# Relative-bias attention and a snake MLP on one core: first loads in another order, and each engine's order of work from a table

## The chip, the core and the metric

The kernel runs on one core of a Trainium2 chip. The core has a matrix engine (TensorE, PE in the profile, with its weight loads on a row of their own, PEld), a vector engine (VectorE, DVE), an engine for activation functions (ScalarE, ACT), a general one (GpSimd, POOL) and one that issues transfers (SyncE, SP). Each engine takes its instructions in the order in which the program holds them, and they meet through semaphores. The metric is device time in microseconds (us), lower is better.

## What is computed

Attention over 8 batches, 8 heads, 576 positions and 64 dimensions, with a bias that depends on the distance of two positions through a table of 32 buckets; its output, seen as 4608 tokens of 512 features, goes through two matrix products with a snake function between them.

```python
scores = scale * np.matmul(q, k.transpose(0, 1, 3, 2))
bucket = np.where(is_small, n, large)          # of n = |i - j|
scores = scores + bias_table[bucket].transpose(2, 0, 1)[None]
attn = np.exp(scores - np.max(scores, axis=-1, keepdims=True))
attn = attn / (np.sum(attn, axis=-1, keepdims=True) + 1e-09)
x = np.matmul(attn, v)                         # heads side by side: 4608 x 512
h = x @ w_in                                   # 512 -> 2048
g = h + np.sin(alpha * h) ** 2 / (alpha + 1e-09)
out = g @ w_out                                # 2048 -> 512
```

## The kernel before

**Attention.** For a batch t the heads are taken in four pairs p. Scores of a pair are matmuls with 64 rows of contraction, the two heads in the two halves of the array (L1069 the main ones, L1059, L1035 and L1030 for the last 64 positions). ACT makes the exponential of 128x1024 scores at a time (`exp_u`, L1076), DVE multiplies in the bias near the diagonal as a factor (`band_t`, L1097; `band_x`, L1081 and L1084), PE multiplies with v over the whole array (`av`, L1111 and L1120), DVE divides by the sum of the exponentials (`norm`, L1130 and L1131). The result is turned into `xT`, in batch 0 by PE (`turn_x_pe`), later by a transposing transfer on SP's queue (`turn_x`, L1137).

**The two products.** The 4608 tokens are cut into nine blocks of 480 to 576, without regard to the batches, so a block needs the finished `xT` of one or two batches. For each block and each of 16 slices of the 2048 features: `moe_in` (four matmuls over the whole array, L1163), the sine on ACT (L1170), square and `g` on DVE (L1174, L1188). Then `moe_out` for each 128 tokens: 16 matmuls (L1197), cut into eight pieces of two, `evict` on DVE (L1203), `store` on SP (L1206). Scores and exponentials of later batches are laid between the pieces of `moe_out`.

**The start.** The first pair of batch 0 comes in halves of its positions: `first_load` (L844) brings two halves of k on SP's queue and two of q on ACT's queue in 32 bit, `first_cast` makes 16 bit of them, `turn_half` turns each on PE with the identity matrix (L990), `half_copy` copies the turned half out of PSUM (L1002, `kT` and `qT`). All other pairs of batches 0 and 1 come on POOL's queue already cast (`load_nat`, L884) and are turned by `turn` (L1010) and copied by `turn_copy` (L1020 on DVE, L1018 on ACT). The bias needs the table (`load_tab`, L863) and constants (`load_consts`, L860); `bias_sub` on PE (L930), `bias_exp` on ACT (L934), `bias_sel` on DVE (L937), four small matmuls (L943), `bias_copy` on ACT (L948), and then eight transfers that spread it out (L958, four on SP's queue, four on POOL's). From batch 2 on, k is written to HBM in 16 bit (L911) and read back transposed (`turn_staged`, L917); of q the same from batch 3.

**What sets the order.** All work is a list of some 1,700 tasks with dependencies, an engine, a duration, and a priority. `_Plan.run` plays it through: whenever an engine is free, it takes from that engine's ready tasks the one of the lowest priority number. The order in which the tasks start in this play is the order in which they are emitted, and so each engine's fixed order of instructions; PSUM banks are given out on the way. Tasks of a named sequence (`seq`) keep the order in which they were added.

The lines on which the start depends, in `_graph`:

```python
first[kind][half] = add("ACT" if kind else "SP", 0.45, E("first_load", kind, half),
                        lat=3.4 if half else 2.95, prio=-9 + 0.3 * half)
t_id = add("SP", 0.45, E("load_ident"), lat=2.7, prio=-8.9)
t_cst = add("ACT", 0.45, E("load_consts"), lat=4.4, prio=-8)
t_tab = add("SP", 0.45, E("load_tab"), lat=4.0, prio=-8)
```

Of the kernel before, what the change touches and what calls it, by code (L numbers as in the profile page):

```python
# [117 lines left out]
class _Plan:  # L118
# [8 lines left out]
    def __init__(self):  # L127
        self.tasks = []
        self.nseq = {}
        self.banks = _Banks()  # L130
        self.fill = None
        self.FILL = 0.0

    def add(self, *a, **kw):
        t = _Task(*a, **kw)
        t.idx = len(self.tasks)
        if not t.lat and not t.pipe:
            t.lat = self.LAT.get(t.eng, 0.0)
        if t.seq is not None:
            t.sn = self.nseq.get(t.seq, 0)  # L140
            self.nseq[t.seq] = t.sn + 1
        self.tasks.append(t)
        return t
# [33 lines left out]
    def run(self):  # L177
# [4 lines left out]
        nxt_seq = {}  # L182
# [11 lines left out]
        n = len(self.tasks)  # L194
        order = []
        while n:
            moved = False
            nxt = None
            for e, cand in pool.items():
# [4 lines left out]
                for t in cand:  # L204
                    if t.seq is not None and nxt_seq.get(t.seq, 0) != t.sn:
                        continue
# [48 lines left out]
                t = best  # L255
# [23 lines left out]
                cand.remove(t)  # L279
                for a in after.get(t.idx, ()):  # L280
                    left[a.idx] -= 1
                    if not left[a.idx]:
                        pool[a.eng].append(a)
# [48 lines left out]

def _graph(K, opt):
    plan = _Plan()
    plan.FILL = opt["fill"]
    plan.fill = lambda m, i: K.fill(m, i)
# [18 lines left out]
    for half in range(2):  # L355
        for kind in range(2):
            first[kind][half] = add("ACT" if kind else "SP", 0.45, E("first_load", kind, half),
                                    lat=3.4 if half else 2.95, prio=-9 + 0.3 * half)
    t_id = add("SP", 0.45, E("load_ident"), lat=2.7, prio=-8.9)
# [148 lines left out]
    def turn_first():  # L508

        done = [[None, None], [None, None]]  # L510
        for half in range(2):
            for kind in range(2):
# [3 lines left out]
                a.emit = lambda a=a, cell=cell, kind=kind, half=half: K.turn_half(cell, tag(a), kind, half)  # L516
                act = (kind, half) in opt["h_act"]
# [10 lines left out]
    def turn(t, p):  # L528
        cell = {}
        for kind in range(2):  # L530
# [5 lines left out]
            a.emit = lambda a=a, kind=kind: K.turn(cell, tag(a), t, p, kind)  # L536
            act = kind and t == 0 and p in opt["turn_act"] or t and (p, kind) in opt["act1"]
# [216 lines left out]
    c_act=((1, 1),), h_act=(), p_bias=-0.5, nu=12, ng=3, first=(1, 1, 1), bs=2, win=7, hold={3:  # L754
# [9 lines left out]
class _Ops:  # L764
# [91 lines left out]
    def load_ident(self):  # L856
        self.nc.sync.dma_start(out=self.ident, in_=self.ident_h.ap())
# [401 lines left out]
```

## Time and profile before

| what | value |
|---|---|
| time, three runs | 393.79, 396.3 and 396.61 us, median 396.3 |
| span of the profiled execution, first to last instruction | 391.7 us |
| TensorE clock granted over the span | 0.994 of full speed |
| busy in the span: PE, DVE, ACT, POOL | 374.0, 301.1, 279.8, 86.4 us |
| matmuls of `moe_in` and `moe_out` | 640 and 576 |
| exponentials of 128x1024 | 160, 154.4 us on ACT |

The profile doesn't say which of the three times belongs to the profiled execution. Its span lies 2.1 us under the lowest and 4.6 us under the median; what lies around the span is between these.

How to read it: busy time of PE is modelled for the ends of matmuls, which overlap, so a stretch that shows 100% may still have small gaps. In the chain of waits a piece runs from the start of its instructions to the start of the next piece, so a gap shows there as a longer piece.

### The profile page before, as it was taken

The page shows a single profiled execution, that of the slowest core. Times are in us where ns is not written, and L with a number is a line of the kernel's source. Part 1 is how long each engine was busy: PE and PEld are TensorE (multiplying, and loading weights), DVE is VectorE, ACT ScalarE, POOL GpSimd, SP SyncE. Part 2 cuts the span into 40 slices and gives each one's busy share as a digit, 9 for nine tenths or more (in the row PEclk, how much of TensorE's full clock was granted, in tenths as well). Part 3 has the DMA queues.
Part 4 walks back from the last instruction along what each step waited for, and adds up shares of the span by engine and source line. Part 5 has one row for each costly group of instructions (what it writes and reads, how often), then busy time and mean ns, then how long its engine had stood idle before and what let it go on. Part 6 is the DMA issues. An engine that isn't in the chain of part 4 may idle for free.

```text
span 391.7 us, 9363 instructions
## 1 busy us (share of the span) xinstructions
PE 374.0 (95%) x3811; PEld 201.1 (51%) x3811; DVE 301.1 (77%) x738; ACT 279.8 (71%) x339; POOL 86.4 (22%) x101
## 2 busy tenths in 40 slices
PE   3979979999999999999999999999999999999996
PEld 2557435565446545564466445644664454444442
DVE  6498797777987798769976997798669889778221
ACT  2888876989689978887789769987897964333000
POOL 8695744080008000900080004000000000000000
PEclk9999998999999999999999999999999999999999
DMA  9999999999549924997499329600211001101122
GB/s 165 197 170 183 195 184 149 145 170 165 82 97 168 176 14 91 165 167 57 89 179 153 34 66 204 74 19 28 64 44 42 30 19 46 36 27 56 54 82 80
DMA packets 148171, 40.80 MB, mean 104 GB/s; under 512 B 134416, under 2 KB 143456, under 8 KB 148128
## 3 DMA queue, kind: packets, MB, share of 16 engines
q0 software_dynamic: 96656, 18.45, 57.7%
q1 hardware_dynamic: 50912, 21.25, 27.9%
q8 instruction: 30, 0.49, 0.5%
q10 hardware_dynamic: 560, 0.50, 0.4%
q14 instruction: 13, 0.11, 0.1%
HBM read 36.94 MB, written 15.93 MB: 135 GB/s over the span
## 4 chain that ended last, share of the span: by engine, by line
PE 88%; DVE 8%; DMA 2%; ACT 1%; issue 1%; SPq 0%
PE acc L1197 33%; PE acc L1163 29%; PE acc L1120 9%; PE acc L1069 9%; DVE g L1188 3%; PE acc L1111 2%; PE acc L1030 2%; PE acc L1059 2%; DMA toep<-in_k_dram 2%; DVE u L1097 1%; DVE s L1174 1%; PE acc L1010 1%; PE acc L1035 1%; DVE xp L1131 1%; DVE qT L1020 1%
## 5 line engine op out<-in xcount | busy, mean ns | idle before, releaser
L1076 ACT ACTIVATE u<-acc 128x1024 f16<-128x1024 f32 x160 | 154.4, 1024 | 21.2 <-PE acc L1069 9.7
L1197 PE MATMUL acc<-w_out,g 128*128 128x512 f16 x576 | 142.9, 381 | 0.0
L1163 PE MATMUL acc<-xT,w_in 128*128 128x512 f16 (+2 forms) x640 | 131.5, 358 | 0.0
L1170 ACT ACTIVATE s<-acc,alphaT 128x512 f16<-128x512 f32 (+2 forms) x144 | 96.2, 687 | 48.5 <-DVE g L1188 26.7
L1188 DVE SCALAR_TENSOR_TENSOR g<-s,inv_a,acc 128x512 f16<-128x512 f16 (+4 forms) x176 | 106.1, 643 | 1.6
L1163 PEld LDWEIGHTS <-w_in 128*128 128x128 f16 x640 | 58.8, 98 | 66.6 <-DVE g L1188 1.4
L1197 PEld LDWEIGHTS <-g 128*128 128x128 f16 x576 | 50.1, 98 | 56.0 <-issue 9.2
L1097 DVE TENSOR_TENSOR u<-u,toep 128x256 f16<-128x256 f16 (+1 forms) x128 | 61.0, 489 | 19.2 <-ACT u L1076 19.0
L1174 DVE TENSOR_TENSOR s<-s 128x512 f16<-128x512 f16 (+2 forms) x144 | 55.5, 417 | 6.1 <-ACT s L1170 6.1
L890 POOL DMA_DIRECT2D v<-in_v_dram x32 | 28.4, 900 | 143.6 <-PE acc L1120 135.8
L1120 PE MATMUL acc<-v,u 128*128 128x65 f16 x1280 | 54.6, 193 | 1.2 <-DVE u L1097 1.2
L1120 PEld LDWEIGHTS <-u 128*128 128x128 f16 x1280 | 50.0, 97 | 5.5 <-DVE u L1097 1.7
L1069 PE MATMUL acc<-qT,kT 64*128 64x256 f16 x512 | 45.1, 280 | 2.4 <-DVE g L1188 1.9
L1203 DVE COPY outs<-acc 128x512 f32<-128x512 f32 x36 | 24.7, 687 | 22.6 <-PE acc L1197 22.3
L1131 DVE TENSOR_TENSOR xp<-acc,rden 128x256 f16<-128x256 f32 (+1 forms) x64 | 31.4, 491 | 2.4 <-DVE rden L1130 0.3
L1069 PEld LDWEIGHTS <-kT 64*128 64x128 f16 x512 | 19.1, 96 | 24.6 <-issue 21.7
L1130 DVE RECIPROCAL rden<-acc 128x4 f32<-128x4 f32 (+1 forms) x64 | 12.0, 187 | 21.5 <-PE acc L1120 21.1
L1111 PE MATMUL acc<-vt,u 128*128 128x130 f16 x128 | 28.2, 221 | 0.0
L1111 PEld LDWEIGHTS <-u 128*128 128x128 f16 x128 | 12.5, 97 | 5.9 <-issue 2.1
L911 POOL DMA_DIRECT2D staged_q<-in_q_dram x5 | 13.9, 2783 | 0.0
L911 POOL DMA_DIRECT2D staged_k<-in_k_dram x6 | 13.6, 2259 | 0.7 <-DMA xT<-in_q_dram 0.7
L1059 PE MATMUL acc<-qT,kT 64*128 64x64 f16 x256 | 9.6, 195 | 2.8 <-ACT u L1076 0.9
(61 smaller groups left out, 166.6 us busy)
## 6 DMA issues: line engine op xcount, KB each, us to landing
out_dram<-outs SPq DMA_DIRECT2D x36, 256.0 KB, 2.0
v<-in_v_dram POOLq DMA_DIRECT2D x32, 128.0 KB, 6.7
staged_k<-in_k_dram POOLq DMA_DIRECT2D x6, 576.0 KB, 11.4
staged_q<-in_q_dram POOLq DMA_DIRECT2D x5, 576.0 KB, 15.4
w_in<-in_moe_w_in_dram POOLq DMA_DIRECT2D x4, 512.0 KB, 8.8
w_out<-in_moe_w_out_dram POOLq DMA_DIRECT2D x4, 512.0 KB, 9.6
xT<-in_q_dram POOLq DMA_DIRECT2D x11, 144.0 KB, 7.0
xT<-in_k_dram POOLq DMA_DIRECT2D x7, 144.0 KB, 6.2
```

Of the source, the lines that this page charges most:

```text
L890: self.nc.gpsimd.dma_start(out=self.vs[t % 2][:, c, :, 0:D], in_=src)
L1069: self.nc.tensor.matmul(out=s[:, o:o + 256], lhsT=self.kT[t % 2][r, p, 128 * c:128 * c + 128], rhs=self.qT[t % 2][r, p, 256 * w:256 * w + ...
L1076: self.nc.scalar.activation(out=c["u"], in_=c["s"], func=AF.Exp, scale=0.125)
L1097: self.nc.vector.tensor_tensor(out=io, in0=io, in1=m, op=ALU.mult)
L1111: nc.tensor.matmul(out=c["av"][:, 130 * j:130 * j + 130], lhsT=tail, rhs=vt[:, p, :], start=True, stop=True, skip_group_check=True)
L1120: nc.tensor.matmul(out=c["av"][:, 130 * j + 65 * a:130 * j + 65 * a + 65], lhsT=l, rhs=vv[:, ch, 2 * p + a, 0:65], start=False, stop=True, ...
L1131: self.nc.vector.tensor_tensor(out=self.ap(x, 256 * w, [[64, n], [1, 64]]), in0=self.ap(av, 0, [[65, n], [1, 64]]), in1=self.ap(r, 0, [[1, ...
L1163: self.nc.tensor.matmul(out=c["h"][:, x:y], lhsT=self.w_in[:, j, 128 * f:128 * f + 128], rhs=self.xT[:, j, lo + x:lo + y], start=(j == 0), ...
L1170: self.nc.scalar.activation(out=c["s"], in_=c["h"], func=AF.Sin, scale=self.alphaT[:, f:f + 1])
L1174: self.nc.vector.tensor_tensor(out=c["s"], in0=c["s"], in1=c["s"], op=ALU.mult)
L1188: self.nc.vector.scalar_tensor_tensor(out=o, in0=c["s"][:, x:y], scalar=self.inv_a[:, f:f + 1], in1=c["h"][:, x:y], op0=ALU.mult, op1=ALU.add)
L1197: self.nc.tensor.matmul(out=c["mo"], lhsT=self.g[b][:, f, 128 * (tau % 4):128 * (tau % 4) + 128], rhs=self.w_out[:, f, :], start=(f == 0), ...
```

## The change

Three things are changed. First, the queues of the start: the identity matrix is loaded on ACT's queue ahead of the halves of q, and the two halves of k stand directly behind one another on SP's queue. Two assumed latencies in the plan go with it, and dependencies are added between the turning of batch 0 and the loads of batch 2 that overwrite the same memory. Second, `_Plan.run` can be given a line: a tuple of all task numbers, and then each engine takes its tasks in the order in which they stand there, whatever their priority; a task that is not yet ready holds up its engine. Third, such a line is given for all tasks, as a text of differences between successive numbers. The arithmetic, the sizes and the number of instructions on each engine stay as they were, but for the one transfer that goes from SP's queue to ACT's.

```diff
@@ class _Plan
+        self.line = ()
@@ def run(self)
+        line = {}
+        for i in self.line:
+            line.setdefault(self.tasks[i].eng, []).append(i)
+        at = dict.fromkeys(line, 0)
...
                 for t in cand:
-                    if t.seq is not None and nxt_seq.get(t.seq, 0) != t.sn:
+                    if line:
+                        if line[e][at[e]] != t.idx:
+                            continue
+                    elif t.seq is not None and nxt_seq.get(t.seq, 0) != t.sn:
                         continue
...
+                if line:
+                    at[e] += 1
@@
+LINE = """
+0 2 4 1 14 1 345 -162 123 228 -274 84 -18 -46 -10 267 -146 333 -350 112 -196 119 123 195 -129 -35
...
+"""
@@ def _graph(K, opt)
+    plan.line = opt["line"]
...
-                                    lat=3.4 if half else 2.95, prio=-9 + 0.3 * half)
-    t_id = add("SP", 0.45, E("load_ident"), lat=2.7, prio=-8.9)
+                                    lat=3.6 - 0.4 * kind if half else 2.95, prio=-9 + 0.3 * half)
+    t_id = add("ACT", 0.45, E("load_ident"), lat=2.7, prio=-9.5)
...
+                if T_nat[2][0][kind] is not None:
+                    T_nat[2][0][kind].deps.append(a)
...
+            if not t and T_nat[2][p][kind] is not None:
+                T_nat[2][p][kind].deps.append(a)
@@ OPT
-    c_act=((1, 1),), ...
+    line=_line(LINE), c_act=((1, 1),), ...
@@ def load_ident(self)
-        self.nc.sync.dma_start(out=self.ident, in_=self.ident_h.ap())
+        self.nc.scalar.dma_start(out=self.ident, in_=self.ident_h.ap())
```

The lines of the operations move down by 79 with it: L1020 becomes L1099, L1076 becomes L1155, L1137 becomes L1216, L1163 becomes L1242, L1197 becomes L1276, and so on.

Three places show what moves. The first is the start on DVE, behind its memsets. `kT_65` and `qT_67` are the turned k and q of even batches, `kT_66` and `qT_68` of odd ones; copies of 288 columns are the halves of the first pair, copies of 576 a whole pair. PE turns the pieces in nearly the order of these copies. Before:

```order
L854 COPY xT<-toep 96x2x192 x2
L1002 COPY kT_65<-acc 128x288
L1002 COPY qT_67<-acc 128x288
L854 COPY xT<-toep 96x2x192
L1002 COPY qT_67<-acc 128x288
L1002 COPY kT_65<-acc 128x288
L1020 COPY kT_65<-acc 128x576
L937 TENSOR_TENSOR eb<-e_83,cst_sb 128x32
L1020 COPY kT_66<-acc 128x576
```

And after:

```order
L933 COPY xT<-toep 96x2x192 x3
L1081 COPY kT_65<-acc 128x288
L1099 COPY kT_65<-acc 128x576
L1081 COPY kT_65<-acc 128x288
L1081 COPY qT_67<-acc 128x288
L1099 COPY kT_66<-acc 128x576
L1016 TENSOR_TENSOR eb<-e_83,cst_sb 128x32
```

All three casts on DVE now come first, and the whole second pair of k comes between the two halves of the first, ahead of the first half of q; on PE the order is first half of k, k of the second pair, first half of q, `bias_sub`, second half of k, k of batch 1's first pair, second half of q, and then the first scores.

The second place is ACT, from the first exponentials to the switch of its table for the first sine. `e_sb` is the bias, the copies to `qT_67`, `kT_66` and `qT_68` are `turn_copy`. Before:

```order
L1076 ACTIVATE u<-acc 128x1024 x2
L948 ACTIVATE e_sb<-acc 128x392
L1076 ACTIVATE u<-acc 128x1024 x8
L1043 ACTIVATE us_75<-acc 128x256
L1076 ACTIVATE u<-acc 128x1024 x7
L1018 ACTIVATE kT_66<-acc 128x576
L1076 ACTIVATE u<-acc 128x1024 x4
L1018 ACTIVATE kT_66<-acc 128x576 x2
L1076 ACTIVATE u<-acc 128x1024 x2
L1018 ACTIVATE qT_68<-acc 128x576
L1076 ACTIVATE u<-acc 128x1024 x3
```

And after:

```order
L1155 ACTIVATE u<-acc 128x1024 x2
L1027 ACTIVATE e_sb<-acc 128x392
L1097 ACTIVATE qT_67<-acc 128x576
L1155 ACTIVATE u<-acc 128x1024 x9
L1122 ACTIVATE us_75<-acc 128x256
L1155 ACTIVATE u<-acc 128x1024 x8
L1097 ACTIVATE kT_66<-acc 128x576
L1155 ACTIVATE u<-acc 128x1024 x2
L1097 ACTIVATE kT_66<-acc 128x576 x2
L1155 ACTIVATE u<-acc 128x1024
L1097 ACTIVATE qT_68<-acc 128x576
L1155 ACTIVATE u<-acc 128x1024 x4
```

The copy to `qT_67` stood ahead of the first exponential and now stands behind `e_sb`; the first copy to `kT_66` (third pair of the loads of batch 1) has two more exponentials ahead of it, and the copy to `qT_68` has four behind it instead of three.

The third place is SP, from the last transposed load of batch 3 to those of batch 4. `kT1` and `qT1` are k and q of batch 3, `kT0` and `qT0` of batch 4; `xT<-xp` are finished tiles of batch 2, which block 2 of `moe_in` waits for. Before, `xp_1644`, `xp_1743` and `xp_1986` are its pairs 1, 2 and 3 (pair 0 stands further ahead):

```order
L1137 DMA_TRANSPOSE xT_77<-xp_1644 128x5x128
L1137 DMA_TRANSPOSE xT_77<-xp_1743 128x5x128
L917 DMA_TRANSPOSE qT1_68<-staged_q 128x4x576
L1206 DMA out_0_dram<-outs_1942 128x512
L917 DMA_TRANSPOSE kT0_65<-staged_k 128x4x576
L917 DMA_TRANSPOSE qT0_67<-staged_q 128x4x576
L1137 DMA_TRANSPOSE xT_77<-xp_1986 128x5x128
```

And after, where `xp_1662`, `xp_1535`, `xp_1757` and `xp_2056` are its pairs 1, 0, 2 and 3:

```order
L996 DMA_TRANSPOSE qT1_68<-staged_q 128x4x576
L1216 DMA_TRANSPOSE xT_77<-xp_1662 128x5x128
L996 DMA_TRANSPOSE kT0_65<-staged_k 128x4x576
L1216 DMA_TRANSPOSE xT_77<-xp_1535 128x5x128
L1285 DMA out_0_dram<-outs_2009 128x512
L1285 DMA out_0_dram<-outs_1975 128x512
L1216 DMA_TRANSPOSE xT_77<-xp_1757 128x5x128
L1216 DMA_TRANSPOSE xT_77<-xp_2056 128x5x128
L996 DMA_TRANSPOSE qT0_67<-staged_q 128x4x576
```

All four tiles of batch 2 now stand behind the q of batch 3, and three of them behind the k of batch 4; the last one stands ahead of the q of batch 4 instead of behind it.

More of the change, by code (lines that the diff above doesn't have):

```diff
@@ L194, in run @@
         n = len(self.tasks)
+        line = {}
+        for i in self.line:
+            line.setdefault(self.tasks[i].eng, []).append(i)
+        assert not line or sorted(self.line) == list(range(n))
+        at = dict.fromkeys(line, 0)
         order = []
@@ L330, with _line @@
 _PENDING = _Pending()
+def _line(text):
+    out, i = [], 0
+    for x in text.split():
+        i += int(x)
+        out.append(i)
+    return tuple(out)
+LINE = """
[50 rows of a table added]
+"""
 def _graph(K, opt):
@@ L753 @@
 OPT = dict(
-    c_act=((1, 1),), h_act=(), p_bias=-0.5, nu=12, ng=3, first=(1, 1, 1), bs=2, win=7, hold={3:
+    line=_line(LINE), c_act=((1, 1),), h_act=(), p_bias=-0.5, nu=12, ng=3, first=(1, 1, 1), bs=2, win=7, hold={3:
     0}, early_mo=False, mo_n=8, ins={-1: {16: 16}, 0: {}, 1: {5: 16}, 2: {15: 16}, 7: {15: 12,
```

49 rows, old and new, of the table LINE are left out of this document.

## The prediction

> **What bounds the kernel now.** I read the page first, then the waits, the chain of waits, and the start and some short stretches in order of time.
>
> ```profile
> span 391.7 us, 9363 instructions
> PE acc L1120 <- DVE u L1097: 0.4, 1, 0.4
> ```
>
> The second row is all that the view of waits has for PE between 60 us and 388 us: one wait, 0.4 us. From 60 us on PE sets the end, and nothing can be gained there but the small gaps inside its own work, and the clock. Before that three stages follow one another. The chain through the first:
>
> ```profile
> 1.68 5.97 DMA toep<-in_k_dram
> 13.78 1.03 ACT u L1076
> 57.55 1.32 DVE g L1188 x2
> ```
>
> The second half of the first k is issued at 1.68 and takes 5.97 us to land; PE and then ACT hang on it. From 13.78 to the first sine, ACT with its exponentials is the one that the others wait for. From there to 59 us the chain is DVE's, square and `g` of block 0 in turn; the change neither adds nor removes work of DVE there, so I cost that stage at nothing: its end moves with its beginning.
>
> **The start, up to the first scores.** The rows in order of time, then transfers with the median time to landing, then PE's steps before:
>
> ```profile
> 0.74 0.93 ACTq L844 DMA_DIRECT2D toep<-in_q_dram  x2
> 1.29 0.77 POOL L884 DMA_DIRECT2D xT<-in_k_dram  x1 [0.84 <-POOLq L1243]
> 1.70 0.47 ACTq L860 DMA_DIRECT2D cst_sb<-cst  x1
> 2.67 0.66 POOL L884 DMA_DIRECT2D xT<-in_k_dram  x1
> ...
> xT<-in_k_dram POOLq DMA_DIRECT2D x2, 144.0 KB, 6.2
> toep<-in_q_dram ACTq DMA_DIRECT2D x2, 144.0 KB, 3.5
> cst_sb<-cst ACTq DMA_DIRECT2D x1, 196.0 KB, 5.6
> ```
>
> ```profile
> 8.08 0.45 PE L990 MATMUL acc<-ident,xT 96*64 96x96 f16 x6 [2.18 <-DVE xT L854]
> 8.33 0.68 PE L1010 MATMUL acc<-ident,xT 96*64 96x96 f16 x12
> 8.94 0.59 PE L930 MATMUL acc<-tab,cst_sb 32*128 32x8 f32 x2
> 9.46 0.69 PE L1010 MATMUL acc<-ident,xT 96*64 96x96 f16 x12
> 10.09 1.04 PE L1069 MATMUL acc<-qT,kT 64*128 64x256 f16 x8
> ```
>
> The halves of q, directly behind one another, take 3.5 us, so k's second half, now in the second place on SP's queue, should land at about 1.2 + 3.5 = 4.7 us instead of 7.65. That stall goes; the question is what is late next. On PE the second thing is now the k of the second pair, from POOL's queue: 1.29 + 6.2 = 7.5 us and everything behind it waits, the first half of q too. Behind it, with the steps of PE's rows (0.25 for a half, 0.61 for a whole pair, 0.52 for L930): half of q 8.1; `bias_sub` 8.35, whose constants (one place of 0.47 later on ACT's queue, 2.17 + 5.6 = 7.8) are there; half of k 8.9; k of batch 1, landed at 2.67 + 6.2 = 8.9, from 9.15; second half of q 9.75; scores at 10.0. They need the first half of q copied, and DVE has put the copy of the second pair (8.2 to 9.0) and of k's half (9.35 to 9.8) ahead of that, so 10.3. Before it was 10.09. **The stall that is removed is replaced by one on POOL's loads: no gain, some 0.2 us lost.**
>
> **ACT from there to the first sine.**
>
> ```profile
> 10.20 0.65 ACT L1018 ACTIVATE qT<-acc 128x576 f16<-128x576 f16 x1 [0.45 <-PE acc L1010]
> 10.75 1.94 ACT L1076 ACTIVATE u<-acc 128x1024 f16<-128x1024 f32 x2
> 12.56 0.51 ACT L948 ACTIVATE e_sb<-acc 128x392 f16<-128x392 f32 x1
> 13.78 7.44 ACT L1076 ACTIVATE u<-acc 128x1024 f16<-128x1024 f32 x8 [0.71 <-PE acc L1035]
> 24.82 3.90 ACT L1076 ACTIVATE u<-acc 128x1024 f16<-128x1024 f32 x4 [0.47 <-ACT u L1076]
> 30.38 0.65 ACT L1018 ACTIVATE kT<-acc 128x576 f16<-128x576 f16 x1 [1.65 <-PE acc L1010]
> 40.70 1.02 ACT L1076 ACTIVATE u<-acc 128x1024 f16<-128x1024 f32 x1 [0.28 <-PE acc L1035]
> ```
>
> Before, the first exponential starts 0.66 after the first scores, and the third 13.78. After: 10.3 + 0.66 to 1.04 (four or all eight matmuls), two exponentials 1.94, bias 0.51, the moved copy 0.65: the third starts at 14.1 to 14.45, 0.3 to 0.7 later; I take 0.5. What comes back: the longest wait, 1.65 us ahead of the first copy to `kT`, has two more exponentials put ahead of it, 2 x 7.44 / 8 = 1.86 us, and should go. The last exponential, which ended at 40.70 + 1.02 = 41.72, then ends at 41.72 + 0.5 - 1.65 = 40.6. What is late next is the last load of batch 1:
>
> ```profile
> 27.38 0.63 POOL L884 DMA_DIRECT2D xT<-in_q_dram  x1
> xT<-in_q_dram POOLq DMA_DIRECT2D x1, 144.0 KB, 7.2
> ```
>
> It lands at 34.6, and at 35.1 or so after the change: POOL's queue stands behind the eight transfers of the bias, which start with `e_sb`, now about 13.1 instead of 12.56. Then 0.69 to turn it, 0.65 to copy, and the four exponentials that ACT has behind that copy, 3.7: 40.1 at the earliest. So the gain at the first sine is at most 1.6 us, by the waits 1.1; a new wait of a few tenths in so tight a row is likely, and it could all be lost. I take **0.8 us gained** (0 to 1.6).
>
> **PE's own gaps from 60 us on.** Pieces of the chain between 127 and 132 us:
>
> ```profile
> 127.47 0.43 PE acc L1197 x2
> 127.90 0.54 PE acc L1069 x8
> ...
> 129.85 0.32 PE acc L1069 x4
> ...
> 130.61 0.06 PE acc L1111
> 130.67 0.24 PE acc L1120 x8
> ...
> 131.53 0.54 PE acc L1197 x2
> ```
>
> Two L1197 behind other whole-array work take 0.43, behind L1069 0.54; four more L1069 cost 0.22, so the first four, 0.32, hold 0.10 too. A change between the split array (64 rows) and the whole one costs about 0.105 us. Counted along the whole order of PE from the first L1197 on, there are 150 such changes before and 140 after: 10 x 0.105 = **1.05 us gained**. The one wait of 0.4 us is at a `band_t` on DVE whose neighbours are reordered; it may stay: 0.2 gained (0 to 0.4).
>
> **Block starts against the finished tiles.** Block 2's first `moe_in` waits for four tiles of batch 2. The last one before, and what stood behind it on PE:
>
> ```profile
> 118.17 1.97 SPq L1137 DMA_TRANSPOSE xT<-xp  x1
> xT<-xp SPq DMA_TRANSPOSE x1, 7.3
> 131.91 1.03 PE L1163 MATMUL acc<-xT,w_in 128*128 128x512 f16 x4
> ```
>
> It landed at 125.5, 6.4 us ahead of its use. In the order of after, PE has between the last product of that tile and block 2 five pieces of L1197 (0.43 each), four groups of scores (0.54 and more) and ten groups of L1111 with L1120 (0.06 + 0.24 each): 2.2 + 2.2 to 3.0 + 3.0, some 8 us. The tile needs `norm` on DVE, perhaps a place on SP behind another tile (up to 2.0), and 7.3: from under 8 to about 10. So PE may wait there 0 to 2 us, and similarly at other blocks while POOL still loads. A quiet transfer would make it nothing. I put **0.5 us lost** over all (0 to 3).
>
> **The sum.** -0.8 - 1.05 - 0.2 + 0.5 = -1.55 us. The profiled span of 391.7 becomes 390.2; its own time is not known, but lies between 393.8 and 396.6. Taken off the median of 396.3, 394.8 us.
>
> **The rivals.** *The dip of the clock goes.* A wait of PE at the end of block 0, the four microseconds soon after it, and four matmuls at their end and four a little later:
>
> ```profile
> 58.26 0.39 PE L1069 MATMUL acc<-qT,kT 64*128 64x256 f16 x4 [1.59 <-DVE g L1188]
> 59.00:63.00 4.00, 3.97 (x45) 1.99 (x45) 3.86 (x8) 3.91 (x6) 4.00 (x2) 0.57 1.66 143
> 61.52 1.63 PE acc L1197 x4
> 63.74 0.86 PE acc L1197 x4
> ```
>
> In the second row the clock is the number ahead of the last two: 0.57 over the four. PE had been waiting for DVE's `g`, and four matmuls then cost 1.63 instead of 0.86. 4 x (1 - 0.57) is 1.7 us of full speed lost, of which the four matmuls alone show 0.77; so 0.8 to 1.7 us hang on it. The Trainium skill, "TensorE: Matmul & The Clock Gate", section "Part 1: The HAM clock gate (the "warmup" mystery)", says that the clock is halved after an idle window of about 3.4 us and freed after a busy one, and that these windows run free of the kernel. The trace agrees: 1.7 us lost at half speed would be such a window. By that rule a shift of a microsecond, or two `turn`s laid elsewhere, can remove the dip or bring one in at another wait. With it gone (-1.2) and the start at its best (-0.8 more) the time is 396.3 - 1.55 - 2.0 = 392.8; chance 0.25. For it: the work on PE near 55 us is regrouped. Against it: DVE still limits block 0, so PE's idle time there has the same sum.
>
> *The gains don't arrive.* ACT carries its 0.5 us and meets a late load, and the waits at the blocks take back the switches: 396.3; chance 0.17.
>
> *Slower: blocks wait for their tiles.* Three tiles of batch 2 now stand behind the k of batch 4 on SP. If the transfers take the 7.3 us that they took under POOL's loads, and blocks 1 to 5 each wait 1.2 us: 5 x 1.2 = 6 us against 2.05 gained by the others, and one more dip of the clock at such a wait, 0.8: 396.3 + 4.7 = 401. It decides from where a tile takes over 8 us from its product to its landing. Against it: from 250 us on little is loaded, and there nothing of this happens. Chance 0.08.
>
> **How the numbers follow.** The forecast, 394.8, has 0.5. The range of 391.6 to 398.0 holds it with its bounds (-3.05 with all terms at their best, +1.8 with the start at 0 and the tiles at their worst) and most of the first two rivals; the three times before lie 2.8 us apart, which widens it at the lower end. One per cent is 4.0 us, about what a measurement of this kernel tells from no change. Faster by more than that needs 392.3 or less: half of the first rival and a little of the forecast's edge, 0.17. Slower: the last rival, 0.08. Within: 0.75.
>
> **What would show it.** Right: the second half of k lands before 5.5 us, PE's third turn starts at 7.5 or later behind a wait for `xT<-in_k_dram`, and the first scores at 10.1 to 10.6; no wait over 0.5 us ahead of the first copy to `kT_66`; the table of the first sine at 40.1 to 41.7; PE's waits behind 60 us under 1 us in sum. Wrong: scores before 9.8 (POOL's loads land earlier when k is out of their way), a sum of waits of PE over 2 us behind 60 us, or a clock under 0.9 in other stretches than this one.

## The result, and the profile after

| kernel | runs | median, us | lowest to highest, us | ratio to before, 95% interval |
|---|---|---|---|---|
| before, beside the change | 4 | 395.14 | 393.79 to 396.61 | |
| changed | 4 | 391.55 | 390.80 to 392.58 | 0.9899, 0.9857 to 0.9940 |
| changed, once more | 6 | 390.52 | 389.61 to 391.48 | 0.9830, 0.9795 to 0.9865 |
| changed, a third time | 6 | 390.70 | 389.62 to 392.59 | 0.9860, 0.9828 to 0.9893 |

The change makes the kernel 1.0 to 1.7% faster, 3.6 to 6 us at the medians; forecast were 1.5 us, and 391.55 lies just under the range. Over all comparisons below, 107 runs of before have the median 396.47 and the 16 of the changed kernel 390.85. The profiled execution of the changed kernel took 391.27 us, with a span of 389.4: 2.3 us less than the span of before. So the profiles differ by less than the medians do, and that is the first thing to explain.

The start, in order of time, with the median times to landing behind it:

```profile
1.15 0.98 ACTq L923 DMA_DIRECT2D toep<-in_q_dram  x2
1.29 0.77 POOL L963 DMA_DIRECT2D xT<-in_k_dram  x1 [0.84 <-POOLq L1322]
7.43 0.69 PE L1089 MATMUL acc<-ident,xT 96*64 96x96 f16 x12 [0.74 <-DMA xT<-in_k_dram]
8.75 0.56 PE L1009 MATMUL acc<-tab,cst_sb 32*128 32x8 f32 x2 [0.39 <-DMA cst_sb<-cst]
10.61 0.79 PE L1148 MATMUL acc<-qT,kT 64*128 64x256 f16 x5
```

```profile
toep<-in_k_dram SPq DMA_DIRECT2D x2, 144.0 KB, 3.4
toep<-in_q_dram ACTq DMA_DIRECT2D x2, 144.0 KB, 5.0
cst_sb<-cst ACTq DMA_DIRECT2D x1, 196.0 KB, 6.5
```

The halves of k now take 3.4 us in the middle, those of q 5.0 instead of 3.5: the late transfer has moved from one queue to the other. PE's second turn waits for the load of POOL's queue until 7.43, and the first scores come at 10.61 instead of 10.09.

ACT up to the first sine:

```profile
24.34 7.51 ACT L1155 ACTIVATE u<-acc 128x1024 f16<-128x1024 f32 x8 [0.43 <-PE acc L1148]
31.71 0.68 ACT L1097 ACTIVATE kT<-acc 128x576 f16<-128x576 f16 x1
40.88 1.28 ACT L1249 ACT_TABLE_LOAD   x1
```

The wait of 1.65 us ahead of the first copy to `kT` is gone, and the table load of the sine starts at 40.88; it was 41.74 in before. That is 0.86 us of gain.

PE at the end of block 0, and the stretch behind it (us; busy time and instructions of PE, PEld, DVE, ACT, POOL; granted clock; DMA share; GB/s):

```profile
55.07 0.70 PE L1089 MATMUL acc<-ident,xT 96*64 96x96 f16 x24 [0.51 <-DMA xT<-in_q_dram]
...
58.10 0.39 PE L1148 MATMUL acc<-qT,kT 64*128 64x256 f16 x4 [1.93 <-DVE g L1267]
```

```profile
58.00:63.00 5.00, 4.69 (x60) 2.26 (x59) 4.15 (x9) 4.29 (x6) 4.09 (x3) 0.66 1.53 132
```

PE waits there as before, and the clock dips as before: 5 x (1 - 0.66) = 1.7 us of full speed are lost. The first `moe_out` starts at 61.32 instead of 61.45, but the dip lies elsewhere against it: of its loss, 1.25 us fall ahead of the first `moe_out` here (3.22 us at 0.61 behind 58.10), and 1.02 in before (2.05 us at 0.50 behind 59.40). The view of waits has nothing at all for PE between 60 and 388 us.

From there on the span can be cut at two places at which exactly the same work of PE lies behind in both orders: the first matmul of the first `moe_out`, and that of the eighth. Two rows of before, then two of after, the second stretch of each up to the end of the last `moe_out`:

```profile
61.45:148.76 87.31, 86.81 (x985) 47.52 (x982) 70.47 (x177) 72.42 (x87) 20.12 (x17) 0.99 1.34 127
148.76:387.91 239.15, 239.15 (x2119) 123.23 (x2117) 182.05 (x436) 160.99 (x195) 23.26 (x22) 1.00 0.56 77
```

```profile
61.32:147.20 85.88, 85.88 (x983) 47.60 (x982) 68.91 (x175) 72.72 (x86) 20.93 (x18) 0.99 1.40 121
147.20:385.67 238.47, 238.47 (x2118) 123.50 (x2116) 180.28 (x440) 159.97 (x195) 23.25 (x22) 1.00 0.60 80
```

So of the 2.24 us between the two profiles, 0.13 lie ahead of the first `moe_out`, 1.43 between it and the eighth, 0.68 behind that. PE shows as busy all through in the last rows, yet one is shorter: busy time of PE is modelled and hides gaps of a tenth.

### The profile page after: what moved, and what is told of

It reads as the page before. It is cut to its first block, busy times and chain, and to the rows that moved or that the text cites. A ratio compares the mean times of both kernels' runs of the same rounds, so it can differ in the third digit from the quotient of the medians.

```text
span 389.4 us, 9321 instructions
## 1 busy us (share of the span) xinstructions
PE 372.6 (96%) x3811; PEld 202.0 (52%) x3811; DVE 297.2 (76%) x738; ACT 279.6 (72%) x339; POOL 85.8 (22%) x101
## 4 chain that ended last, share of the span: by engine, by line
PE 85%; DMA 11%; POOL 2%; DVE 1%; issue 0%; ACTq 0%; ACT 0%; SPq 0%; POOLq 0%
PE acc L1276 33%; PE acc L1242 28%; PE acc L1199 9%; PE acc L1148 8%; DMA xT<-in_q_dram 4%; DMA w_in<-in_moe_w_in_dram 2%; PE acc L1190 2%; PE acc L1109 2%; DMA v<-in_v_dram 2%; DMA cst_sb<-cst 2%; PE acc L1138 1%; DMA toep<-e_sb 1%; POOL xT L963 1%; PE acc L1089 0%; POOL mt L1042 0%
## 5 line engine op out<-in xcount | busy, mean ns | idle before, releaser
L1155 ACT ACTIVATE u<-acc 128x1024 f16<-128x1024 f32 x160 | 154.6, 1026 | 19.4 <-PE acc L1148 15.3
L1276 PE MATMUL acc<-w_out,g 128*128 128x512 f16 x576 | 145.9, 381 | 0.0
L1242 PE MATMUL acc<-xT,w_in 128*128 128x512 f16 (+2 forms) x640 | 134.9, 358 | 0.0
L1267 DVE SCALAR_TENSOR_TENSOR g<-s,inv_a,acc 128x512 f16<-128x512 f16 (+4 forms) x176 | 107.5, 646 | 1.5
L1242 PEld LDWEIGHTS <-w_in 128*128 128x128 f16 x640 | 59.0, 98 | 67.0 <-issue 0.7
L1276 PEld LDWEIGHTS <-g 128*128 128x128 f16 x576 | 50.8, 98 | 53.9 <-issue 8.1
L1253 DVE TENSOR_TENSOR s<-s 128x512 f16<-128x512 f16 (+2 forms) x144 | 57.2, 420 | 16.8 <-ACT s L1249 16.5
L1176 DVE TENSOR_TENSOR u<-u,toep 128x1024 f16<-128x1024 f16 (+1 forms) x128 | 58.9, 486 | 14.3 <-ACT u L1155 13.8
```

The source lines that it names most:

```text
L1155: self.nc.scalar.activation(out=c["u"], in_=c["s"], func=AF.Exp, scale=0.125)
L1176: self.nc.vector.tensor_tensor(out=io, in0=io, in1=m, op=ALU.mult)
L1242: self.nc.tensor.matmul(out=c["h"][:, x:y], lhsT=self.w_in[:, j, 128 * f:128 * f + 128], rhs=self.xT[:, j, lo + x:lo + y], start=(j == 0), ...
L1253: self.nc.vector.tensor_tensor(out=c["s"], in0=c["s"], in1=c["s"], op=ALU.mult)
L1267: self.nc.vector.scalar_tensor_tensor(out=o, in0=c["s"][:, x:y], scalar=self.inv_a[:, f:f + 1], in1=c["h"][:, x:y], op0=ALU.mult, op1=ALU.add)
L1276: self.nc.tensor.matmul(out=c["mo"], lhsT=self.g[b][:, f, 128 * (tau % 4):128 * (tau % 4) + 128], rhs=self.w_out[:, f, :], start=(f == 0), ...
```

## The experiments

All mixed orders use the table of the changed kernel with other numbers in it; POOL's order is the same in both kernels. In the expectations, "before" stands for the runs of the kernel before in the same comparison.

### Which execution was the profile of before?

The kernel before, unchanged.

> The kernel before, once more, with a profile, to see which of its times belong to the profiled execution. Theory A (wrong base): its times fall in two groups some 2.5 us apart, about 393.9 and 396.4, and a profile with a span near 391.7 belongs to the lower group, so that the fair difference to the changed kernel is about -2.3 us, not the -3.6 of the medians. Theory B: the times scatter evenly, and a span of 391.7 can go with 396.3 too (more than 4 us around the span).

Measured: 12 runs, median 396.30, from 393.78 to 399.68, with no gap in the middle; what lies around the span is the same in all 107 runs of before, 1.72 to 1.93 us. So the profile of the forecast, span 391.7, belongs to an execution of about 393.5 us, under the three times that were known and one of the fastest there are. Neither theory was right in its form: the times are no two groups, but the base was wrong by about 3 us. What the new profile, span 393.3, has more shows on DVE and on PE:

```profile
117.42 0.68 DVE L1097 TENSOR_TENSOR u<-u,toep 128x1024 f16<-128x1024 f16 x1
119.52 0.94 DVE L924 COPY kd<-kT 64x256 f16<-64x256 f16 x2 [1.42 <-DMA kT<-staged_k]
```

```profile
119.57 0.23 PE L1120 MATMUL acc<-v,u 128*128 128x65 f16 x2
120.84 0.35 PE L1120 MATMUL acc<-v,u 128*128 128x65 f16 x6 [1.05 <-DVE u L1097]
121.44 0.81 PE L1197 MATMUL acc<-w_out,g 128*128 128x512 f16 x3 [0.24 <-DVE outs L1203]
```

The corner copy of batch 4 (L924, which copies the last 64 positions of k into `kd`) stands on DVE where its k just lands. DVE waits 1.42 us, the multiplication behind the copy comes late, and PE waits 1.05 and 0.24. In the profile of the forecast the same copy has no wait:

```profile
117.45 0.68 DVE L1097 TENSOR_TENSOR u<-u,toep 128x1024 f16<-128x1024 f16 x1
118.05 0.72 DVE L924 COPY kd<-kT 64x256 f16<-64x256 f16 x2
```

The transfer, issued at 112.84, took 5.16 us there and landed at 118.00, 0.05 us ahead of the copy; here it took 6.69. The list of waits has nothing at this place (its one row of the kind, 1.0 us, is the copy of batch 5 at 158.55, in the stretch that takes 239.15 us in either profile); the landing and the start of the copy side by side show it.

### Queues and order, each alone

```diff
 queue_only: identity first on ACT's queue, halves of k together
-LINE = the changed order
+LINE = the order of before on every engine
 order_only: the changed order
-    t_id = add("ACT", ...)      # and nc.scalar.dma_start
+    t_id = add("SP", ...)       # and nc.sync.dma_start, between the halves of k
```

> The queues of the change (identity first on ACT's queue, the halves of k directly behind one another) with every engine's order of before. Theory A (the gain lies behind 61 us): within 0.4 us of before; the second half of k lands near 5.5, but the second half of q takes its place as the late one, near 7.7, so the first scores start at 10.0 to 10.3 as before. Theory B (the start gives the gain): the first scores start at 9.6 or earlier and the time is 0.8 us or more under before.

> Every engine's order of the change with the queues of before (identity on SP's queue between the halves of k). Theory A: the whole gain of the change, 2.0 to 2.5 us under before, since the queues give nothing. Theory B: at most half of it, 0 to 1.2 us under before.

Measured: queue_only 396.47 us against 396.00, ratio 0.9993 (0.9969 to 1.0018); order_only 392.37, ratio 0.9894 (0.9859 to 0.9929). The order gives most of the gain, 3.6 us and so more than theory A said, and the queues by themselves none; what they add to the new order is not measured (0.9894 here, 0.9830 to 0.9899 for the changed kernel). But the first scores of queue_only start at 9.61, not at 10.0 to 10.3: the queues do something that theory A denied. The first load of POOL's queue, issued at 1.29 or 1.30 in either case, lands at 6.59. In ten profiles with the new queues it lands between 5.93 and 7.57 (middle 6.4), in nine with the old ones between 7.46 and 8.94 (middle 7.8). The profile of the changed kernel, 7.38, is the second-latest of the ten.

### The start alone, the rest alone

```diff
 start_new: changed queues
+LINE = the changed order up to the first moe_out, then the order of before
 rest_new: queues of before
+LINE = the order of before up to the first moe_out, then the changed order
```

> The change (queues and order) up to the first piece of moe_out, and behind it the order of before on every engine. Theory A: the first sine's table load at 40.9 as in the changed kernel, 0.8 us earlier than before, but the first L1276 at 61.2 to 61.4, and the time within 0.3 us of before: the gain of the start is eaten at the end of block 0. Theory B: the 0.8 us reach the end, time 0.8 us or more under before.

> The reverse of the earlier split: queues and order of before up to the first piece of moe_out, the order of the change behind it. Theory C with the switches of the array: 2.1 us (1.05 for ten switches, 1.07 for the gaps that went) and the late loads, together 2.5 to 3.5 us under before. If the start gave half of the gain, as the split with the new start showed (1.9 us), this one should show the other half only, 1.7 to 2.5 us.

Measured: start_new 394.11 us against 396.00, ratio 0.9951 (0.9921 to 0.9982); rest_new 393.21 against 396.49, ratio 0.9894 (0.9859 to 0.9930). So the start gives 1.9 us and the rest 3.3, as its expectation had it (2.5 to 3.5), and the two make up about the whole. Theory A of start_new, which I had drawn from the two profiles (0.86 us gained at the first sine, 0.13 left at the first `moe_out`), is wrong: in the profile of start_new the first `moe_out` starts at 59.66. Two things had misled me.

The first is the place of the dip. Two later profiles with the same start, after_again and after_tight, have the first `moe_out` at 59.86 and 59.68, with none of the dip's loss ahead of it; a third, after_third, has 61.48, with 3.5 us at half clock ahead of it. The wait of 0.51 us for `xT<-in_q_dram` in the profile of the changed kernel stands ahead of one of 1.93 for DVE, and no run shows that it costs anything.

The second is that the start, too, was early in the two profiles of before. Five profiles have the order and the queues of before up to the first sine and no matmul added ahead of it; its table load starts at 41.74 and 41.58 (before and before_again), 43.38 (before_corners, with a dip at 27 to 30 us), 43.56 (rest_new) and 44.69 (before_fill_b0). In the eight with the changed start it comes at 39.67 to 41.27. The number of dips is not what start_new gains by: its runs of a clock of 0.993 or more have a median of 393.45 us against 395.03 of before beside it, the others 394.98 against 396.62, 1.6 us in either group.

### Corner copies where k just lands

```diff
 before_corners: DVE's order of before
-band_t, corners(4), band_t, evict, band_t, ...
+band_t, band_t, evict, band_t, ... 25 tasks of DVE ..., corners(4)      # and so for batches 3, 5, 6, 7
 after_tight: DVE's order of the changed kernel
-band_t, evict, ... , corners(4)
+band_t, corners(4), evict, ...                                       # and so for batch 7
```

> The changed kernel once more, as the measure for the others here. Theory C (late loads on DVE's queue: before, the corner copies L924 of batches 4 and 5 stand where k just lands, 0.05 and 0.02 us of slack in the profile, so that in many runs DVE and then PE wait a microsecond or more; the change puts them elsewhere): the median lies 3.6 to 4.4 us under before's although the profiles differ by 2.3, and its runs lie closer together than before's. Theory D (the runs differ only by the clock's dip near 60 us): the spread is as wide as before's, and the difference of the medians is the 2.3 us of the profiles.

> The kernel before with one thing moved: on DVE the corner copies (L924 there) of batches 3 to 7 stand 25 places of DVE's work later, still over 25 places ahead of their first use. Theory C: no wait for kT<-staged_k is left at these copies, no gap over 0.3 us on PE between 118 and 122 us, and the median is 0.8 to 2 us under before's. Theory D: the median stays within 0.4 us of before's.

> The changed kernel with the corner copies of batches 4 and 7 put back on DVE to where k just lands: ahead of the two evictions that start at 115.62 and 235.56 us in the profile of the changed kernel, where k lands at 115.10 and 234.38. Theory C (a copy that stands where its load just lands costs time in the mean, whatever one profile shows): median 0.5 to 1.5 us over the changed kernel, and in a profile a wait for kT<-staged_k at these copies or none. Rival: DVE idles over 1.6 us at both places, so a late k is hidden; within 0.3 us.

Measured: after_again 390.52 us against 396.49, 5.97 us less and so more than either theory said; 1.87 us between its lowest and highest run of 6, where 16 of before have 5.17. before_corners 395.42, 1.07 us less than before, but with an interval that touches no change (0.9948 to 1.0004). The profiles are clearer. From the first `moe_out` to the eighth, six profiles that have DVE's order of before take 87.31 (the one of the forecast), 88.69, 89.08, 89.11, 89.22 and 89.35 us (before_fill_b0, whose end of block 0 is another, 88.96). In each but the first DVE waits 1.1 to 1.4 us at this copy, and PE then 1.0 to 1.6 us behind it. What else separates them is the place of the dip: without its loss in this stretch (0.7 to 1.6 us) the first has 86.6 and the others 87.6 to 88.3. before_corners takes 87.67, 87.1 without the dip, and no wait for `kT<-staged_k` is left in it, nor in the changed kernel. But its edit takes back half a microsecond: ahead of two matmuls of `moe_in`, at 102.7 and 104.7 us, PE has gaps of 0.31 and 0.26 where before has 0.09 and none. So the price of the copy is read from the profiles, and no median shows it clear of noise. The profile on which I forecast was the one that had been spared.

after_tight is a miss: 390.65 us, the same as the changed kernel beside it (390.70). Its list of waits (us in total, times, longest) has the wait for k again, and before_fill18 below, with the order of before, has nearly the same row:

```profile
DVE kd L1010 <- DMA kT<-staged_k: 1.3, 1, 1.3
```

```profile
DVE kd L924 <- DMA kT<-staged_k: 1.2, 1, 1.2
```

But in after_tight no gap of PE over 0.15 us follows: at these places DVE had rested 1.67 and 1.75 us anyhow. A copy where its load just lands costs only where DVE has no rest behind it.

### The price of a change between split and whole array

```diff
 switch_more: PE's order of the changed kernel, at five places behind the fourth moe_out
-scores, piece of moe_out, ...
+piece of moe_out, scores, ...      # so that one more pair of changes arises
```

> The changed kernel with five pairs of neighbours swapped on PE behind the fourth moe_out, so that there are ten more changes between the split array and the whole one. Price of a change 0.105 us: the span from the first matmul of the fifth moe_out to the last one, 275.1 us in the changed kernel, becomes 276.1 to 276.3. If a change costs nothing by itself: 275.0 to 275.3.

From the eighth `moe_out` on, in which all ten changes lie:

```profile
145.56:385.83 240.27, 239.70 (x2118) 122.66 (x2116) 180.79 (x440) 160.53 (x195) 23.27 (x22) 1.00 0.57 80
```

240.27 instead of 238.47, where nine other profiles of the changed order behind the first `moe_out` have 238.45 to 238.47. Of the 1.80 us, 0.74 is one gap between two matmuls that the trace puts down to no other engine and that the nine do not have:

```profile
207.65 0.28 PE L1116 MATMUL acc<-qT,kd 128*128 128x256 f16 x1
208.50 0.28 PE L1116 MATMUL acc<-qT,kd 128*128 128x256 f16 x1 [0.57 <-issue]
```

The other 1.06 by ten are 0.106 us for one change. The stretch of the expectation, from the fifth `moe_out` on, takes 276.93, over the 276.1 to 276.3, and 276.19 without that gap; so the price is as forecast if the gap, whose cause is open, has nothing to do with the changes. The two kernels bear it out: in the stretch from the eighth `moe_out` on before has 96 changes and the changed kernel 88, so 0.85 of gain was to be expected; the changed order has one wait for DVE's `g` of 0.16 in it (at 183.7) that before has not, and the 0.69 that this leaves are there (0.68). The Trainium skill, "TensorEngine Tiling (Array Packing)", section "Key Properties", says that a change of the tiling mode drains the engine, without a price; the drain itself is not seen in the trace, but its price would be these 0.106 us.

### The end of block 0 and the clock

```diff
 both_early: PE's order of the changed kernel at the end of block 0
-scores, scores, turn, scores, turn, scores, moe_out 0 ...
+scores, six pieces of moe_out 0, scores, scores, scores, scores, turn, ..., turn, ...
 after_fill62
-    fill=0
+    fill=62                   # 62 matmuls on zeros in PE's gaps up to there
 after_fill_b0
+    fill=62, and only from 45 on   # the 20 of them that lie in the wait at the end of block 0
```

> The changed kernel with PE's wait at the end of block 0 filled: the first six pieces of moe_out (features 0 to 1535, whose g is there) are put ahead of the group of scores that waits 1.93 us for DVE, and the turning of the last two pairs of batch 2 (and DVE's two copies) behind it. Theory E (PE's wait there and the half clock that follows are what eats the gain of the start): the wait of 1.93 us goes, the clock stays at 1.00 from 58 to 63 us, and the time is 2 to 3 us under the changed kernel. Theory F (ACT and DVE, busy over 0.95 from 56 to 60 us, set the pace): the waits come back behind the pieces and the time is within 0.7 us of the changed kernel.

> The changed kernel with 62 small matmuls on zeros in PE's gaps up to the end of block 0, 20 of them in the wait there. Theory E (the half clock behind the wait at the end of block 0 costs about 1 us): the clock of most runs is 0.999 or 1.0, the first moe_out starts by 59.5, and the time is 0.5 to 1.5 us under the changed kernel's median of 390.5. Theory F: moe_out waits for other things; the time is within 0.4 us or longer by the added matmuls.

> The changed kernel as the measure for the three others on this chip: median 390 to 391.6, clock 0.994 or more in at least three of four runs.

> The changed kernel with 20 small matmuls on zeros in PE's wait at the end of block 0 and none at the start. Theory E (the half clock behind that wait costs about 1 us, and the added matmuls of the start had eaten this in the run before): clock 0.999 or 1.0 in most runs, median 0.6 to 1.3 us under the changed kernel. Theory F (ACT sets the pace up to 66 us): clock up, time within 0.3 us.

Measured: both_early 391.62 us (six runs), no better than the changed kernel. Its first `moe_out` starts 5.85 us earlier, at 55.47, and its eighth at 147.16, as in the changed kernel (147.20): what has been moved waits now for ACT's exponentials, 2.6 us between 59 and 68 us, and the dip comes at 62 to 66:

```profile
PE acc L1152 <- ACT u L1159: 2.1, 2, 1.4
...
PE acc L1142 <- ACT u L1159: 0.5, 1, 0.5
```

So theory F holds for this edit. after_fill62: clock 1.000 in all six runs, but 391.33 us; its first sine comes at 41.65, where the eight profiles of the changed start without matmuls added ahead of it have 39.67 to 41.27. after_fill_b0 adds none there: 389.30 us (388.29 to 390.04, clock 0.998 or more in all five runs) beside 390.70 of the changed kernel, ratio to before 0.9818 (0.9791 to 0.9844). One row of the third profile of the changed kernel, which has two dips one behind the other, and one of after_fill_b0:

```profile
58.00:65.00 7.00, 6.75 (x66) 2.86 (x66) 5.21 (x10) 5.07 (x6) 3.92 (x2) 0.51 2.13 153
```

```profile
58.00:63.00 5.00, 5.00 (x93) 2.89 (x90) 4.85 (x9) 5.00 (x7) 4.42 (x2) 1.00 1.76 156
```

Seven microseconds at 0.51 are 3.4 of full speed lost, against none. So for the clock theory E holds: twenty matmuls on zeros in block 0's wait remove the dip, and the medians lie 1.4 us apart. In that difference is the second dip of two of the six runs of the changed kernel; the median of its other four is 389.7. This kernel is faster than both, by 1.8% than before.

### The second dip

The mean clock of a run tells how many dips it has: in the profiles 0.994 to 0.996 goes with one of 1.7 us, 0.989 to 0.991 with two, 0.999 or more with none. Of the 107 runs of before 65 are under 0.993, with a median of 396.83 against 395.01 of the others; of the 16 of the changed kernel 4 are (392.53 against 390.59). So at the same number of dips the change is worth 4.3 to 4.4 us, and the rest of the 5.6 between the medians is that fewer runs have two. Where the second one lies is not the same in all profiles: behind the first in order_only, after_third and before_both, and in before_corners in the attention of batch 0:

```profile
26.00:31.00 5.00, 4.53 (x80) 3.73 (x80) 2.88 (x12) 3.38 (x4) 5.00 (x8) 0.66 1.12 160
60.00:65.00 5.00, 4.74 (x64) 2.57 (x62) 4.50 (x9) 4.55 (x6) 3.31 (x2) 0.66 1.94 155
```

Four kernels were to show what brings it, all from before:

```diff
 before_fill30 / before_both
+    fill=30                   # 54 matmuls on zeros up to there; before_both has the late corner copies too
 before_fill18
+    fill=30, and only from 17.5 on   # 22 of them
 before_fill_b0
+    fill=62, and only ahead of two tasks at the end of block 0   # 28 of them
```

> The kernel before, with 54 small matmuls on zeros (128x256, results read by nobody) put into PE's gaps before the end of the attention on batch 0. Theory G (in many runs the clock is halved for a second stretch of 3.4 us at 23 to 30 us, because PE rests three times for about a microsecond there; the new order has fewer such rests, so the stretch comes less often): the clock of most runs is 0.994 or more where before has 0.991 or less in more than half of its runs, and the median falls by 1 to 2 us. Theory H (the clock falls whatever PE does there): the clocks are spread as before, the time is the same or up to 1 us longer by the added matmuls.

> The kernel before with the 54 small matmuls and with the corner copies 25 places later on DVE. Theories C and G together: 1 us by the copies and 1 to 2 us by the clock, median 2 to 3 us under before, the runs within 2 us of one another. If either falls, 1 us or less under before.

> The kernel before with 22 small matmuls on zeros, all in the gaps of PE between 17.5 and 30 us, none ahead of that. Theory G (PE's three rests of about a microsecond there bring the second stretch of half clock): at most a quarter of the runs has a clock under 0.993, against 51 of 80 of the kernel before, and the median falls by 0.8 to 1.6 us. Theory H (it comes from elsewhere): more than half of the runs under 0.993, median within 0.5 us of before's.

> The kernel before with 28 small matmuls on zeros in its two waits at the end of block 0 (before the group of scores that waits 1.75 us for DVE, and one place ahead), none elsewhere. Theory I (both stretches of half clock come at the end of block 0, one behind the other, because PE waits there): nearly all runs have a clock of 0.998 or more, and the median falls by 1.5 to 2.5 us. Theory J (the second stretch comes from the start): about two thirds of the runs keep one stretch, clock 0.994 to 0.996, the median falls by 0.7 to 1.3 us.

Measured: before_fill30 397.49 us, before_both 397.45, before_fill18 396.88, none faster than before beside it (396.54, 396.54, 396.73). Runs under 0.993: 5 of 12, 7 of 12 and 5 of 12, so rather fewer than 65 of 107, but not the quarter that theory G asked for. In these three profiles the first sine comes at 42.8 to 44.5, which is no later than in profiles of the same start without added matmuls (41.58 to 44.69); but the runs of before_fill30 with a clock of 0.993 or more take 2.3 us more than those of before beside it (396.84 against 394.58), so the added matmuls may hide a gain. The theory is neither shown nor refuted. before_fill_b0 missed its aim: its matmuls themselves waited 0.90 us for ACT and held up the scores behind them, the first `moe_out` moved to 69.3 and the time to 402.28 (its first sine, at 44.7, was late already); it says nothing on either theory. What brings the second dip in two of three runs of before, and why the changed order has it in one of four, stays open.

## Why the prediction was wrong

**The base.** The step that failed first is the last of the sum: "Taken off the median of 396.3 us, 394.8 us." The terms were read from a span of 391.7, whose own time is 393.5 (1.7 to 1.9 around the span in every run of before), not 396.3. Off 393.5 the same sum gives 391.95, 0.4 us from the result. That it comes so near is partly luck: the two profiles lie 2.24 us apart and not 1.55, and the terms were off in both directions. The median was no neutral base either: what lies between 393.5 and 396.3 are losses that most executions of before have and the profiled one did not, the late corner copy (1.0 to 1.6 us), a second dip of the clock (1.8 us between the two medians above) and, as far as five profiles tell, a start up to 3 us later. The sum put all of them at nothing. The change moves the corner copy of batch 4 from 118.05 to 148.33 us, 33 us behind the landing of its k, and has two dips in 4 of 16 runs instead of 65 of 107. A term for the copy could have been in the sum: the landing and the copy were both in the trace, 0.05 us apart.

**The start: right in the profile, too small for the other executions.** k's second half landed at 5.45 (forecast under 5.5), PE waited for POOL's load until 7.43 (at its second turn, not its third), the scores came at 10.61 (forecast up to 10.6), the wait ahead of `kT` went, the table load of the sine came at 40.88: the signs stood as forecast within a tenth, and 0.8 us of gain were 0.86. "Its end moves with its beginning" holds within half a microsecond: from that table load to the first `moe_out`, less the dip's loss on the way, it is 18.7 us in before and 19.0 to 19.2 in the changed kernel, start_new, after_again and after_tight. What was too dear is the price of POOL's load: with the new queues it lands at 6.4 in the middle, not at the 7.5 that I took over from before. "Scores before 9.8" was named as a sign of error; five of the ten profiles with the new queues have it (9.54 to 9.72, with the new or the old order). But early scores are not yet the gain: queue_only has them at 9.61 and gains nothing, and with the changed start scores at 9.72 go with a first sine at 41.27 (after_third), scores at 10.94 with one at 40.90 (after_fill_b0). That the start gives 1.6 to 1.9 us is shown by start_new; which of its moved loads and copies does it stays open.

**PE's own gaps: mis-sized.** The price of a change of the array, 0.105, was right (0.106), and ten changes fewer are about 1 us. The term behind it, "the one wait of 0.4 us ... 0.2 gained", was wrong by more: the row of waits shows 0.42 because the ends of matmuls are modelled. Counted from the starts of the matmuls, against the step that is usual between two such matmuls, PE has in before three gaps between 87 and 91 us, 0.15, 0.58 and 0.17, and four of less than 0.1 up to 113; in the changed kernel two of 0.14 are left. 0.2 should have been 0.9. Waits and changes together were forecast at 1.25 and come to 2.0 so; the two profiles differ by 2.1 behind the first `moe_out` (1.43 + 0.68), of which 0.2 are the place of the dip.

**Block starts against the tiles: wrong.** 0.5 us lost was forecast, nothing was lost: PE has no wait behind 60 us in the profile of the changed kernel. The last tile of batch 2 took 5.8 us to land, not 7.3, and was there at 126.40, 1.2 us ahead of block 2's first `moe_in` at 127.58. So the margin shrank from 6.4 us as the argument had it, and was just enough. The slower rival (five waits of 1.2 us) falls with it, and so does the one by which the gains don't arrive.

**The rivals.** "The dip of the clock goes" was the nearest in time (392.8), and wrong as told: the dip at block 0's wait stayed in both profiles. Its rule, that a shift can remove a dip or bring one in, fits runs of one kernel that differ by a dip. What the profiles do not show is a whole window without work ahead of it: in the 3.41 us ahead of the dip PE is busy for 1.26 in the profile of the changed kernel and for 2.20 in after_again. The Trainium skill, "TensorE: Matmul & The Clock Gate", section "Part 1: The HAM clock gate (the "warmup" mystery)", says that the window runs free of the kernel and that the same kernel therefore differs from run to run. The runs agree: one kernel has clocks of 0.989 to 1.000 in six executions (after_third).

## What to carry to other kernels

A profile is one execution: add what lies around its span, see where it stands among the times, and take the sum from its own time; then look for what the other executions have lost, first of all for transfers that land within a few tenths of the instruction that needs them. Here a late load cost time only where the engine that waited had no rest at that place and the bounding engine hung on it. Small gaps of a pipelined engine are counted from the starts of its instructions, not from the view of waits.

## What the runs showed that I had not expected

The stretch from the eighth `moe_out` to the end takes the same time in nearly every profile of one order: 239.15 us in eight of nine profiles with PE's order of before, 238.45 to 238.47 in nine with the changed one. Nearly all that varies between executions lies ahead of it.

With the identity's transfer on ACT's queue and the halves of k together on SP's, the first load of a third queue lands 1.4 us earlier in the middle (6.4 instead of 7.8; 5.93 to 7.57 in ten profiles, 7.46 to 8.94 in nine), although it is issued at the same time. The transfer behind the identity on ACT's queue takes 3.9 us in the profile of the changed kernel and the next one 6.1 (in the ten, 3.0 to 3.9 and 4.5 to 6.1), where they took 3.4 and 3.5 at the head of the queue.

A wait of PE of 1.6 to 1.9 us, with shorter ones beside it, stands at the end of block 0 in fifteen profiles, and fourteen of them have 3.4 us of half clock there or soon after, three of them 6.8; after_tight has the same wait and none. Twenty small matmuls in that wait removed it in all five runs.
